# Moving a weight load and its product forward in the first batches of a Linformer and mixture-of-experts kernel

## The chip, the cores and the metric

One core of a Trainium2 chip runs the whole program. The metric is device time in microseconds (us); less is better.

## The reference

An attention with 32 memory slots feeds a mixture of experts. In short:

```python
a = softmax(phi, over the 32 slots)                  # B, H, S, 32
k_m = einsum('bhsm,bhsd->bhmd', a, k)                # slot sums of the keys
v_m = einsum('bhsm,bhsd->bhmd', a, v)                # and of the values
attn = softmax(q @ k_m.T / sqrt(64))                 # B, H, S, 32
x = (attn @ v_m) as tokens of 512                    # 8 heads x 64
expert = argmax(normalised x @ normalised emb.T / tau); gate = its softmax weight
out = gate * (relu(x @ w1[expert]) @ w2[expert])     # 512 -> 1024 -> 512
```

There are 8 batches of 576 tokens, 8 heads of 64, 8 experts, all in float32.

## The kernel before

The kernel goes batch by batch. For each batch it forms the slot sums of keys and values (a softmax of phi on ScalarE, transposes of it on TensorE, products with the loaded keys and values), then the scores and their softmax, then picks an expert, and then runs the two expert layers. The values are never multiplied out to tokens before the first layer: `project` multiplies the slot values by W1 (products `pg`, 512 hidden columns at a time), and `first` multiplies the attention weights by that projection (products `ph`). Matrix products whose precision matters are split in a high and a low part: `gh` and `gl` of the projection, `ah` and `al` of the weights (tile `aT`), `hh` and `hl` of the hidden layer, `wh` and `wl` of W2.

From batch 0's first layer on, the loops `first` and `second` emit the big products of one batch, and a table (`steps`) hangs the small work of the next batches between them. Ahead of that stands a prologue, written out by hand in `moe_linformer` (from L1104 on). The change touches the prologue alone. Every engine runs its own instructions in the order in which the program emits them, and all loads named here go through one queue that SyncE (SP) issues in order.

The prologue prepares batch 0 completely up to its first layer, and the slot sums of batch 1. The steps that matter here, with the names the rows use:

- `load_kv(1)`: keys and values of batch 1 in two halves of 1024 KB, tiles `kx` 0 and `kx` 1, and the last 64 tokens (`kl`, 256 KB).
- `pick`: the expert of batch 0, guessed from sums, is read into a register of SP; `load_w1(e, 0)` and `load_w1(e, 1)` then load W1 in two halves of 512 columns (tile `w1s`, 1024 KB each).
- `turn(1, g)` and `tails(1)`: transposes of batch 1's softmaxed phi on TensorE (tiles `te`, `tz`), copied out by ScalarE to `eT` and `kt`.
- `slots(1, ...)`: the slot sums (`acc0t`, `acc`) over five pieces of tokens, in the order 0, 1, 4, 2, 3; pieces 0 and 1 read `kx` 0, piece 4 reads `kl`, pieces 2 and 3 read `kx` 1.
- `scale(1)`, `keys(1)`, `values(1)`: ScalarE scales the sums to `ks`, TensorE transposes them (`tk`, `tv`), ScalarE copies them out.
- `project(0, ..., apart=True)`: a generator, driven by `next(project)`. Its first step emits the products `pg` of W1's first half, the next one the copies to `gh` on ScalarE and the subtractions to `gl` on VectorE; the second half follows inside `first`.
- `t.attend()` and `t.turned(...)`: products `po` and transposes `tt` of batch 0, after which the first `ph` comes.
- `warm`: products of ones whose result nobody reads; they stand in TensorE's queue between other steps.

Of the kernel before, what the change touches and what calls it, by code (L numbers as in the profile page):

```python
# [19 lines left out]
P = 128  # L20
# [285 lines left out]
class Kernel:  # L306
# [150 lines left out]
                else:  # L457
                    (self.nc.scalar if b in (3, 4) else self.nc.sync).dma_start(to, self.phiT[b, :, g])

    def load_kv(self, b):  # L460
        if 1 < b < B:
            for g in range(NG):
                to, x = self.kl[64 * g : 64 * g + 64], self.kvt[b, :, 4 * g : 4 * g + 4]
                self.nc.sync.dma_start(to, x)
        if b < B:
            for k in range(2):
                if b < 2 and k:
                    x = self.kvt[b].rearrange("t (g j) d -> (t g) (j d)", g=NG)
                    self.nc.sync.dma_start(self.kl.rearrange("p j d -> p (j d)"), x)
                self.nc.sync.dma_start(self.kx[k], self.kv[b, :, 2 * k : 2 * k + 2])  # L470

    def load_q(self, b, halves=(0, 1)):
        if b < B:
# [280 lines left out]
    def project(self, n, vT, room=None, apart=False):  # L754

        nc = self.nc
        for k in range(2):
            ps = [(room or self.mm)([P, 512], f"pg{n}_{k}{g}") for g in range(NG)]
            for g, j, r, c, i in self.heads():
                f = slice(512 * k, 512 * k + 512)  # L760
                nc.tensor.matmul(ps[g][j], lhsT=vT[r, g, c % 2, i], rhs=self.w1s[r, c, f], start=True, stop=True)
            f = slice(512 * k, 512 * k + 512)
            if apart and not k:
                yield
            for g in range(NG):
                nc.scalar.copy(self.gh[:, g, f], ps[g])  # L766
            for g in range(NG):
                nc.vector.tensor_tensor(  # L768
                    out=self.gl[:, g, f], in0=ps[g], in1=self.gh[:, g, f].bitcast(F32), op=ALU.subtract
                )  # L770
            yield
# [331 lines left out]
@with_exitstack  # L1103
def moe_linformer(ctx, tc, phiT, qT, kv, kvt, emb, tau, w1, w2, out):  # L1104
    k = Kernel(ctx, tc, phiT, qT, kv, kvt, emb, tau, w1, w2, out)
    ctx.enter_context(tc.manual_schedule(engines={ET.PE, ET.DVE, ET.Activation, ET.SP, ET.Pool}))


    k.eights()
    k.warm(4)  # L1110
    k.warm(8, hot=k.mm([P, 256], "half", 0))
    k.warm(32, hot=k.mm([P, 64], "cool", 0))
    k.load_phi(0)
    k.load_kv(0)
    k.load_q(0, (0,))
    k.load_router()
    k.consts()
    accs = [k.ps.tile([P, 2 * D], F32, tag=f"{n}3", name=f"acc0{n}", bufs=1) for n in "tm"]
    for vT in k.vT:
        k.nc.vector.memset(vT, 0.0)  # L1120
    router = k.router()
    for g in range(NG):
        k.largest(0, g)
        k.softmax(0, (g,))
    for g in range(NG):
        k.turn(0, g)
        if not g:
            next(router)
        k.warm(4 if g else 8, hot=k.mm([P, 256], f"half{g}", 0))
    k.tails(0)  # L1130
    k.shares(0)
    next(router)
    k.load_phi(1, (0,))
    k.load_q(0, (1,))
    k.load_phi(1, (1,))
    t = Tokens(k, 0, k.pt)
    for ks in ((0, 1), (4,), (2, 3)):
        k.slots(0, accs, ks=ks, first=0 in ks, last=3 in ks)
        if 3 not in ks:
            k.warm(4, hot=k.mm([P, 128], f"hot{ks[0]}", 0))  # L1140
    k.scale(0)
    next(router, None)
    k.warm(2, hot=k.mm([P, 128], "hot2", 0))
    k.load_kv(1)
    k.keys(0)
    t.summed()
    k.again()
    values = k.values(0, copy=k.nc.scalar.copy, room=lambda *a: k.mm(*a, 3))
    all, tr, te = slice(0, BL), [k.mm([P, S - 64], f"tr0_{g}", g) for g in range(NG)], [k.mm([P, 64], "te0_0", 2)]
    k.score(0, tr, 64, S, (0,))  # L1150
    t.guess()
    k.score(0, te, 0, 64, (0,))
    next(values)
    t.fill((0,), slice(2, BL), tr)
    e = t.pick()
    t.fill((0,), slice(0, 2), te)
    list(values)
    k.load_w1(e, 0)
    k.load_w1(e, 1)
    k.load_q(1, (0,))  # L1160
    tl = [k.pt([P, D + E], f"tl0_{g}") for g in range(NG)]
    k.squares(0, tl)
    k.score(0, tr, 64, S, (1,))
    te.append(k.pt([P, 64], "te0_1"))
    k.score(0, te, 0, 64, (1,))
    k.products(0, copy=True)
    work = [t.weigh((g,), all, None if g else k.nc.gpsimd) for g in range(NG)]
    next(work[0])
    for g in range(NG):
        k.largest(1, g)  # L1170
    next(work[0])
    t.fill((1,), slice(2, BL), tr)
    t.fill((1,), slice(0, 2), te)
    k.softmax(1, (0,))
    list(work[0])
    k.softmax(1, (1,))
    k.warm(12, hot=k.mm([P, 256], "warm0", 3))
    list(work[1])
    k.turn(1, 0)
    k.warm(12, hot=k.mm([P, 128], "warm1", 3))  # L1180
    k.turn(1, 1)
    k.tails(1)
    k.warm(10, hot=k.mm([P, 128], "warm2", 3))
    k.shares(1, v=k.nc.gpsimd, invert=False)
    project = k.project(0, k.vT[0], apart=True)
    accs = [accs[0], k.mm([P, 2 * D], "acc1", 3)]
    for ks in ((0,), (1,), (4,), (2,), (3,)):
        k.slots(1, accs, ks=ks, first=0 in ks, last=3 in ks)
    t.divide(range(NG), all, True, lambda: k.invert(1))
    k.tags, k.turns = 4, 3  # L1190
    k.scale(1)
    k.again(k.nc.scalar.copy)
    k.keys(1, lambda *a: k.mm(*a, 3))
    list(k.values(1, copy=k.nc.scalar.copy, room=lambda *a: k.mm(*a, 2)))
    next(project)
    t.turn(range(NG), all)
    for g in range(NG):
        k.part(g, slice(0, HS), k.nc.gpsimd.tensor_copy)
    next(project)
    t.attend()  # L1200
    t.turned(0, 1)
    t.turned(4)
    k.load_w2(e)
    k.load_q(1, (1,))
    k.load_phi(2)
    k.second_part = project
    for b in range(B):
        u = Tokens(k, b + 1, k.pt) if b < B - 1 else None
        left = k.batch(b, t, u)
        t = u  # L1210
    k.rest(*left)
# [29 lines left out]
```

## Time and profile before

| | us |
|---|---|
| median of 3 runs | 393.63 |
| lowest and highest | 392.93, 394.96 |
| the profiled execution | 393.70 |
| its span, first to last instruction | 391.9 |
| TensorE busy in the span | 383.1 (98%) |
| VectorE, ScalarE, GpSimd busy | 242.6, 213.1, 190.0 |

The profile is one execution. Its own time is 1.8 us longer than the span of its instructions. Times in rows count from the span's start. PE is TensorE's products, DVE VectorE, ACT ScalarE, POOL GpSimd, SPq the queue of SyncE. A float32 product is two instructions in the trace where the program has one; transposes are one.

### The profile page before, as it was taken

Reading aid. Unit: us, or ns where it says so; the run is one execution under the profiler, and the core shown is the slowest. Engines: PE = TensorE matmul, PEld = TensorE weight load, DVE = VectorE, ACT = ScalarE, POOL = GpSimd, SP = SyncE. Lnnn points to the kernel's source line nnn. Section 1 sums busy time; section 2 is a strip of 40 time slices with the busy share of each in tenths; the row PEclk is TensorE's granted clock in tenths of the full one; section 3 lists DMA queues with packets and bytes.
Section 4 is the critical chain, followed back from the end, with each engine's and each line's share of the span. In section 5 each row is a group of like instructions: output and inputs, shape, how many; then the busy total and the mean of one; then the engine's idle time right before and its main releaser. Section 6 shows DMA issues by size and latency. Waiting matters only on the chain. (4 is left out here: it accounts for less than half of the span.)

```text
span 391.9 us, 10402 instructions
## 1 busy us (share of the span) xinstructions
PE 383.1 (98%) x3890; PEld 313.7 (80%) x3890; DVE 242.6 (62%) x800; ACT 213.1 (54%) x665; POOL 190.0 (48%) x234
## 2 busy tenths in 40 slices
PE   8899999999999999999999999999999999999995
PEld 5568878799787978889787987879787897879783
DVE  5579896679673798259862798538861696445000
ACT  5366734778484875666656675657641751145011
POOL 1165940596154932478052951559242871529300
PEclk9999999999999999999999999999999999999999
DMA  8999827995789937995489926995379205890011
GB/s 307 407 355 359 347 59 191 339 370 225 162 264 369 403 95 151 382 391 200 90 251 378 403 72 155 349 390 210 74 205 386 91 2 103 271 381 2 30 54 44
DMA packets 65447, 91.25 MB, mean 233 GB/s; under 512 B 40712, under 2 KB 45320, under 8 KB 63216
## 3 DMA queue, kind: packets, MB, share of 16 engines
q1 hardware_dynamic: 62016, 81.02, 61.4%
q0 software_dynamic: 2688, 8.26, 5.8%
q10 hardware_dynamic: 688, 1.26, 1.2%
q8 instruction: 32, 0.52, 0.6%
q14 instruction: 23, 0.19, 0.2%
HBM read 71.19 MB, written 19.33 MB: 231 GB/s over the span
## 5 line engine op out<-in xcount | busy, mean ns | idle before, releaser
L784 PE MATMUL ph<-aT,gh 128*128 128x288 f32 x512 | 103.1, 297 | 0.0
L824 PE MATMUL py<-wh,hh 128*128 128x512 f32 x256 | 100.9, 394 | 0.0
L824 PE MATMUL py<-wl,hh 128*128 128x512 f32 x256 | 99.9, 390 | 0.2 <-POOLq L1013 0.2
L824 PE MATMUL py<-wh,hl 128*128 128x512 f32 x256 | 99.9, 390 | 0.0
L751 POOL TENSOR_TENSOR wl<-w2s,wh 128x512 fp32r<-128x512 f32 x64 | 83.2, 1300 | 5.1
L784 PEld LDWEIGHTS ph<-aT,gh 128*128 128x128 f32 x512 | 81.8, 188 | 1.8 <-DVE hl L791 0.8
L784 PE MATMUL ph<-aT,gl 128*128 128x288 f32 x256 | 75.4, 295 | 0.0
L788 ACT ACTIVATE hh<-ph 128x224 fp32r<-128x224 f32 (+1 forms) x128 | 48.8, 388 | 33.7 <-PE ph L784 33.0
L791 DVE SCALAR_TENSOR_TENSOR hl<-ph,hh 128x224 fp32r<-128x224 f32 (+1 forms) x128 | 51.8, 417 | 23.5 <-ACT hh L788 16.9
L829 ACT ACTIVATE ys<-py,gate 128x512 f32<-128x512 f32 (+1 forms) x40 | 25.7, 643 | 63.3 <-PE py L824 33.0
L990 POOL DMA_DIRECT2D out_dram<-ys x28 | 16.2, 580 | 89.6 <-ACT ys L829 89.5
L824 PEld LDWEIGHTS py<-wh,hh 128*128 128x128 f32 x256 | 48.1, 188 | 10.9 <-issue 1.4
L824 PEld LDWEIGHTS py<-wh,hl 128*128 128x128 f32 x256 | 48.1, 188 | 10.2
L824 PEld LDWEIGHTS py<-wl,hh 128*128 128x128 f32 x256 | 48.1, 188 | 10.1 <-POOLq L1013 0.6
L784 PEld LDWEIGHTS ph<-aT,gl 128*128 128x128 f32 x256 | 48.0, 188 | 0.0
L768 DVE TENSOR_TENSOR gl<-pg,gh 128x512 fp32r<-128x512 f32 x32 | 20.0, 684 | 43.4 <-ACT gh L766 43.4
L750 POOL CAST wh<-w2s 128x512 fp32r<-128x512 f32 x62 | 41.3, 665 | 0.9 <-PE ph L784 0.8
L741 POOL TENSOR_TENSOR aT<-aw,aT 128x576 fp32r<-128x576 f32 (+1 forms) x18 | 23.5, 1320 | 34.1 <-DVE aT L740 29.3
L579 ACT COPY eT<-xt 32x256 f32<-32x256 f32 x80 | 32.3, 403 | 1.4
L813 PE MATMUL py<-w2s,h 128*64 128x256 f32 x256 | 29.4, 382 | 0.0
L651 ACT COPY kv<-kt 32x64 f32<-32x64 f32 x96 | 23.3, 243 | 6.6 <-DVE kt L641 5.5
L813 PEld LDWEIGHTS py<-w2s,h 128*64 128x64 f32 x256 | 17.7, 137 | 10.7 <-DVE aw L102 2.1
(184 smaller groups left out, 473.8 us busy)
## 6 DMA issues: line engine op xcount, KB each, us to landing
kx<-kv SPq DMA_DIRECT2D x16, 1024.0 KB, 11.3
w2s<-w SPq DMA_DIRECT2D x28, 512.0 KB, 10.1
w1s<-w SPq DMA_DIRECT2D x28, 512.0 KB, 6.3
qt<-qT SPq DMA_DIRECT2D x14, 576.0 KB, 10.1
out_dram<-ys POOLq DMA_DIRECT2D x28, 256.0 KB, 6.4
ad<-aw SPq DMA_DIRECT2D x8, 576.0 KB, 12.8
td<-x SPq DMA_DIRECT2D x56, 72.0 KB, 2.5
ea<-td SPq DMA_DIRECT2D x7, 512.0 KB, 4.1
```

The lines of the kernel that those rows point to most:

```text
L579: nc.scalar.copy(eT[to, :8, m].rearrange("p (g k) m -> p g k m", g=NG), xt[at, :, q : BL - 2 : 4])
L651: nc.scalar.copy(y, self.kt[32 * l : 32 * l + 32, g, h + 2 * i :: 2 - 4 * i])
L741: self.nc.gpsimd.tensor_tensor(out=al, in0=a, in1=ah.bitcast(F32), op=ALU.subtract)
L750: (copy or self.nc.scalar.copy)(h, x)
L751: self.nc.gpsimd.tensor_tensor(out=l, in0=x, in1=h.bitcast(F32), op=ALU.subtract)
L768: nc.vector.tensor_tensor(out=self.gl[:, g, f], in0=ps[g], in1=self.gh[:, g, f].bitcast(F32), op=ALU.subtract)
L784: nc.tensor.matmul(p, lhsT=w[:, g, fs], rhs=x[:, g, to], start=g == 0 and k == 0, stop=g == 1 and k == 2)
L788: nc.scalar.activation(self.hh[:, f, at], q, AF.Relu)
L791: nc.vector.scalar_tensor_tensor(out=self.hl[:, f, at], in0=q, scalar=0.0, in1=self.hh[:, f, at].bitcast(F32), op0=ALU.max, op1=ALU.subtract)
L813: nc.tensor.matmul(p[64 * j : 64 * j + 64], lhsT=self.h4[:, f], rhs=self.w2s[:, f, d * j : d * j + d], start=f == 0, stop=f == 7,)
L824: nc.tensor.matmul(p, lhsT=h[:, f, to], rhs=w[:, f], start=f == 0 and k == 0, stop=f == 7 and k == 2)
L829: nc.scalar.activation(y[:, :d], p, AF.Copy, scale=gate[:, i : i + 1])
```

## The change

Four things move in the prologue, and one generator gets another step.

- `load_kv` takes the halves to load. Batch 1's `kx` 0 and `kl` are loaded where they were; `kx` 1 is loaded after the pick, behind W1's first half and ahead of its second.
- The products `pg` of W1's first half stand between piece 4 and piece 2 of the slot sums. The copies to `gh` stand behind the slot sums, and the subtractions to `gl` where both stood before.
- The first transposes of batch 1's phi are emitted ahead of the exponential of batch 0's second half of scores, so that ScalarE copies them out sooner.
- Ten `warm` products ahead of the slot sums go.
- Eight opening `warm` products of 256 columns become sixteen of 128.

```diff
-    def load_kv(self, b):
+    def load_kv(self, b, ks=range(2)):
...
         if b < B:
-            for k in range(2):
-                if b < 2 and k:
+            for k in ks:
+                self.nc.sync.dma_start(self.kx[k], self.kv[b, :, 2 * k : 2 * k + 2])
+                if b < 2 and not k:
                     x = self.kvt[b].rearrange("t (g j) d -> (t g) (j d)", g=NG)
                     self.nc.sync.dma_start(self.kl.rearrange("p j d -> p (j d)"), x)
-                self.nc.sync.dma_start(self.kx[k], self.kv[b, :, 2 * k : 2 * k + 2])
...
             for g in range(NG):
                 nc.scalar.copy(self.gh[:, g, f], ps[g])
+            if apart and not k:
+                yield
...
-    k.warm(8, hot=k.mm([P, 256], "half", 0))
+    k.warm(16, hot=k.mm([P, 128], "half", 0))
...
-    k.load_kv(1)
+    k.load_kv(1, (0,))
...
     k.load_w1(e, 0)
+    k.load_kv(1, (1,))
     k.load_w1(e, 1)
...
     k.warm(12, hot=k.mm([P, 256], "warm0", 3))
+    k.turn(1, 0)
     list(work[1])
-    k.turn(1, 0)
     k.warm(12, hot=k.mm([P, 128], "warm1", 3))
     k.turn(1, 1)
     k.tails(1)
-    k.warm(10, hot=k.mm([P, 128], "warm2", 3))
...
     for ks in ((0,), (1,), (4,), (2,), (3,)):
+        if 2 in ks:
+            next(project)
         k.slots(1, accs, ks=ks, first=0 in ks, last=3 in ks)
+    next(project)
...
     list(k.values(1, copy=k.nc.scalar.copy, room=lambda *a: k.mm(*a, 2)))
-    next(project)
     t.turn(range(NG), all)
```

SP's queue, from the load of batch 1's `kx` 0 to W1's second half; `TENSOR_LOAD ai` reads the picked expert. Before:

```order
L470 DMA kx0_70<-kv 128x2048
L469 DMA kl_72<-kvt 128x512
L470 DMA kx1_71<-kv 128x2048
L229 TENSOR_LOAD ai_354
L229 ISA x2
L489 ISA
L489 DMA w1s_87<-w1 128x4x512
L489 ISA
L489 DMA w1s_87<-w1 128x4x512
```

And with the change:

```order
L467 DMA kx0_70<-kv 128x2048
L470 DMA kl_72<-kvt 128x512
L229 TENSOR_LOAD ai_361
L229 ISA x2
L489 ISA
L489 DMA w1s_87<-w1 128x4x512
L467 DMA kx1_71<-kv 128x2048
L489 ISA
L489 DMA w1s_87<-w1 128x4x512
```

The load of `kx` 1 has gone from ahead of the register read to between the two halves of W1.

TensorE, from piece 2 of batch 1's slot sums to the first product of `attend`. Before:

```order
L602 MATMUL acc0t_182<-kx1_71,eT_74 32x128 x4
L602 MATMUL acc1_477<-kx1_71,eT_74 32x128 x4
L602 MATMUL acc0t_182<-kx1_71,eT_74 32x128 x4
L602 MATMUL acc1_477<-kx1_71,eT_74 32x128 x4
L627 MATMUL tk1_0_529<-ident_162,ks_75 128x128 x2
L662 MATMUL tv1_0_533<-ident_162,ks_75 128x128 x2
L761 MATMUL pg0_00_540<-w1s_87,kv20_78 32x512 x4
L761 MATMUL pg0_01_541<-w1s_87,kv20_78 32x512 x4
L133 MATMUL po0_0_562<-vv_80,aw_86 64x72
```

And with the change, from behind piece 4:

```order
L761 MATMUL pg0_00_499<-w1s_87,kv20_78 32x512 x4
L761 MATMUL pg0_01_500<-w1s_87,kv20_78 32x512 x4
L602 MATMUL acc0t_190<-kx1_71,eT_74 32x128 x4
L602 MATMUL acc1_474<-kx1_71,eT_74 32x128 x4
L602 MATMUL acc0t_190<-kx1_71,eT_74 32x128 x4
L602 MATMUL acc1_474<-kx1_71,eT_74 32x128 x4
L627 MATMUL tk1_0_538<-ident_170,ks_75 128x128 x2
L662 MATMUL tv1_0_542<-ident_170,ks_75 128x128 x2
L133 MATMUL po0_0_559<-vv_80,aw_86 64x72
```

The products `pg` have moved from between `tv` and `po` to ahead of the pieces that read `kx` 1.

ScalarE, from the exponential of batch 0's second half of scores (`x`) to the copies to `gh`. Before:

```order
L76 ACTIVATE x_81<-x_81 128x576
L546 COPY eT_74<-te1_0_432 128x512
L546 COPY eT_74<-te1_1_451 128x512
L553 COPY kt_76<-tz1_457 128x256
L619 ACTIVATE ks_75<-acc0t_182,rs1_404 128x128
L619 ACTIVATE ks_75<-acc1_477,rs1_404 128x128
L656 COPY ks_75<-ks_75 128x2x64
L632 COPY kv21_79<-tk1_0_529 128x256
L668 COPY kv21_79<-tv1_0_533 64x2x32 x4
L766 CAST gh_91<-pg0_00_540 128x512
L766 CAST gh_91<-pg0_01_541 128x512
```

And with the change:

```order
L546 COPY eT_74<-te1_0_436 128x512
L76 ACTIVATE x_81<-x_81 128x576
L546 COPY eT_74<-te1_1_459 128x512
L553 COPY kt_76<-tz1_465 128x256
L766 CAST gh_91<-pg0_00_499 128x512
L766 CAST gh_91<-pg0_01_500 128x512
L619 ACTIVATE ks_75<-acc0t_190,rs1_412 128x128
L619 ACTIVATE ks_75<-acc1_474,rs1_412 128x128
L656 COPY ks_75<-ks_75 128x2x64
```

One copy to `eT` has passed the exponential, and the two copies to `gh` have passed the scaling of the slot sums.

## Rows read from the trace of the kernel before

**Rows 1.** Windows, TensorE: stretch, length, busy, granted clock, DMA share, GB/s

```profile
30.42:387.30 356.88, 356.55 (x3441) 1.00 0.68 225
```

**Rows 2.** Timeline of TensorE, prologue's end: start, length, line, operation, idle before

```profile
22.35 0.72 PE L442 MATMUL warm<-ones 128*128 128x128 bf16 x10
23.41 0.43 PE L602 MATMUL acc0t<-kx,eT 128*32 128x128 f32 x8 [0.34 <-ACT eT L546]
23.90 0.42 PE L602 MATMUL acc<-kx,eT 128*32 128x128 f32 x8
...
25.02 0.42 PE L602 MATMUL acc0t<-kx,eT 128*32 128x128 f32 x8
...
26.66 0.44 PE L627 MATMUL tk<-ident,ks 128*128 128x128 f32 x2 [0.56 <-ACT ks L619]
...
27.36 1.09 PE L761 MATMUL pg<-w1s,kv 64*32 64x512 f32 x16
28.38 1.48 PE L133 MATMUL po<-vv,aw 64*64 64x72 f32 x80
...
30.42 0.51 PE L784 MATMUL ph<-aT,gh 128*128 128x288 f32 x2
...
32.17 1.09 PE L761 MATMUL pg<-w1s,kv 64*32 64x512 f32 x16
```

**Rows 3.** Timeline of ScalarE in the same stretch

```profile
22.07 0.68 ACT L76 ACTIVATE x<-x 128x576 f32<-128x576 f32 x1 [0.74 <-DVE x L74]
22.77 1.07 ACT L546 COPY eT<-te 128x512 f32<-128x512 f32 x2
...
25.93 0.37 ACT L619 ACTIVATE ks<-acc0t,rs 128x128 f32<-128x128 f32 x1 [1.81 <-DVE aw L102]
...
28.48 1.07 ACT L766 CAST gh<-pg 128x512 fp32r<-128x512 f32 x2 [0.16 <-PE pg L761]
```

**Rows 4.** Timelines of VectorE and GpSimd: what the first `ph` also needs

```profile
26.71 0.20 DVE L102 STREAM_TRANSPOSE aw<-x 128x64 f32<-128x64 f32 x1
29.11 1.29 DVE L768 TENSOR_TENSOR gl<-pg,gh 128x512 fp32r<-128x512 f32 x2 [2.19 <-ACT gh L766]
...
27.67 0.80 POOL L741 TENSOR_TENSOR aT<-aw,aT 128x288 fp32r<-128x288 f32 x1
```

**Rows 5.** SP's timeline, then DMA issues by window (size, us to landing)

```profile
13.83 0.33 SPq L470 DMA_DIRECT2D kx<-kv  x1
18.47 1.50 SPq L489 DMA_DIRECT2D w1s<-w  x2
...
kx<-kv SPq DMA_DIRECT2D x1, 1024.0 KB, 8.7
...
w1s<-w SPq DMA_DIRECT2D x1, 1024.0 KB, 6.8
...
w1s<-w SPq DMA_DIRECT2D x1, 1024.0 KB, 8.5
```

**Rows 6.** Windows, all engines: last three columns are granted clock, DMA share, GB/s

```profile
1.50:3.70 2.20, 2.14 (x8) 0.91 (x7) 1.34 (x9) 1.49 (x2) 0.27 (x2) 1.00 0.92 275
...
19.70:19.90 0.20, 0.20 (x4) 0.18 (x3) 0.20 (x1) 0.20 (x3) 0.00 (x0) 1.00 0.10 41
19.90:23.10 3.20, 3.17 (x39) 2.73 (x36) 3.04 (x6) 2.43 (x6) 1.67 (x6) 1.00 0.95 342
23.10:25.80 2.70, 2.32 (x78) 2.06 (x80) 2.58 (x7) 1.02 (x3) 1.84 (x3) 1.00 1.05 394
```

**Rows 7.** Timelines: the opening, VectorE's first use of a load, later warm products

```profile
2.97 1.87 PE L442 MATMUL half<-ones 128*128 128x256 bf16 x8
...
9.58 0.65 PE L602 MATMUL acc0t<-kx,eT 128*32 128x128 f32 x16 [0.66 <-DMA kx<-kv]
...
3.67 1.51 DVE L504 TENSOR_REDUCE nm<-ex 128x1 f32<-128x576 f32 x2 [0.83 <-DMA ex<-phiT]
...
19.08 1.49 PE L442 MATMUL warm<-ones 128*128 128x256 bf16 x12
```

## Prediction

> **What bounds the kernel now.** I read the windows first. From the first `ph` at 30.42 us to 387.30 us TensorE is busy 356.55 of 356.88 us [rows 1]: what stands behind 30.42 us is TensorE's own work, none of it changed, and whatever the prologue gains or loses at the first `ph` arrives undiminished at the end. So the question is one number: at what time does the first `ph` start?
>
> The timeline of TensorE around it [rows 2] shows the chain. The slot sums of batch 1 start at 23.41 us, after 0.34 us of waiting for ScalarE's copy `eT`. The second group follows at 23.90, the pieces that read `kx` 1 at 25.02, the transposes `tk` at 26.66 after 0.56 us of waiting for `ks`, `pg` at 27.36, `po` at 28.38 and `ph` at 30.42. All the idle time in it, 0.90 us, is TensorE waiting for ScalarE. ScalarE's timeline [rows 3] gives the other half: it stands idle 0.74 us before the exponential at 22.07, makes two copies to `eT` from 22.77 (1.07 us), scales the first sums at 25.93 and starts `gh` at 28.48, again 1.07 us for two.
>
> The loads come last. `kx` 1 is issued at 13.83 and lands 8.7 us later, at 22.5; the halves of W1 are issued at 18.47 and about 19.4 and land after 6.8 and 8.5 us, at 25.3 and 27.9 [rows 5]. Each is there before TensorE asks for it (25.02 for `kx` 1, 27.36 and 32.17 for the halves of W1 [rows 2]), so no load is on the path now.
>
> **The change, part by part.** *Copy and warm products.* With the first copy to `eT` in the idle 0.74 us ahead of 22.07, only the second is left behind the exponential: it ends about 23.30 instead of 23.84. The first sums no longer wait behind the ten warm products (0.72 us from 22.35 [rows 2]); the second group then starts about 23.37 instead of 23.90, which is 0.53 us sooner. Its two pieces and piece 4 take the 1.12 us that stand between 23.90 and 25.02. TensorE is ready for the moved `pg` at 24.49. Removing the warm products alone is worth nothing, since the copies set this time.
>
> *The product.* `pg` fills 27.36 to 28.38, that is 1.02 us of the queue [rows 2]. It leaves that place and takes the same 1.02 us at 24.49, so that piece 2 could start at 25.51. Behind it, from the start of piece 2 to the scaling on ScalarE stand 0.91 us (25.02 to 25.93), and from there to the end of `tv` 1.43 us (25.93 to 27.36) [rows 2, 3]. `po` then follows at once.
>
> *The copies to `gh`* now stand in ScalarE's queue ahead of the scaling. They can start when `pg` ends: 1.12 us after its start by the rows (27.36 to 28.48). With the 1.07 us that they take, the scaling can't start before 24.49 + 2.19 = 26.68 us. Without any wait for loads the path is therefore: scaling at 26.68, `po` at 28.11, 0.27 us sooner than 28.38. Behind the scaling wait `tk`, `tv` and with them TensorE's whole queue. The subtractions to `gl` follow VectorE's last transpose of `aw`, which ends at 26.91, and take 1.29 us; GpSimd's `al` is done at 28.47 [rows 4]. Both are there before any `ph` considered here (30.1 or later), so they cost nothing; if `gl` lost its 1.9 us of cover it would hold `ph` itself.
>
> *The loads* decide the rest. W1's first half can't be issued sooner, since SP still waits for the pick: 18.47. In the profile of before, the mean DMA share falls to 0.10 from 19.70 to 19.90 and the rate to 41 GB/s [rows 6]: the queue had run dry, so most engines began W1's first half when its issue let them, not when `kx` 1 did. Taking `kx` 1 from ahead of it leaves the DMA engines idle earlier and brings W1's bytes hardly sooner. What it does take away is the tail: `kx` 1 landed at 22.5, 2.6 us after the share had fallen, so a few engines must have run late, and those kept W1's landing at 25.3 too. The bytes themselves (1.05 MB) were through by 23.1 (342 GB/s x 3.2 us = 1.09 MB), and a second 1.05 MB by 25.8 (394 x 2.7 = 1.06 MB) [rows 6]. How soon a load lands behind its last byte when no engine is late is seen at the start: 0.6 MB have moved by 3.7 us (275 GB/s x 2.2 us), as much as the first two loads of phi, and VectorE uses the first of them from 3.67 us [rows 6, 7]; the second reduction can have started by 4.4. That is up to about 0.5 us. So W1's first half lands between 23.2 and 25.3; I take 23.6, before `pg` wants it. Behind it stands `kx` 1 in the place of W1's second half: between 25.6 (no late engine, some rate regained) and 27.9 (late engines stay as late as they were). I take 25.8 + 0.5 = 26.3, since after a pause of more than 2 us in the queue the late ones should have caught up.
>
> By the Trainium skill ("DMA: Bandwidth & Descriptors", section on why a DMA increments its semaphore by 16 and not by 1) a load counts as landed only when the last of its up to 16 engines has finished. The gap between the idle share at 19.8 and the landing at 22.5 agrees with it.
>
> *Sum.* Piece 2 starts at 26.35, the scaling at 26.35 + 0.91 = 27.26, `po` at 27.26 + 1.43 = 28.69. Against 28.38 that is 0.31 us later. `ph` moves from 30.42 to 30.73, the span from 391.9 to 392.2, the profiled 393.70 to 394.0. The median of the runs shown is 0.07 us below the profiled time, so I predict **393.9 us**. In short: the reordering is worth 0.27 us, and TensorE gives it back by waiting 0.8 us for `kx` 1.
>
> *What is hidden.* W1's second half lands 2.6 us behind `kx` 1, about 28.9 and 30.5 at worst, before 32.17. Everything SP issues behind it moves by one issue of 0.33 us at most, and the bytes by about 1 us; I see no use of them that stands closer than W1's second half. Sixteen opening products of 128 columns have as many columns as eight of 256; if each cost 0.03 us of its own more, the first transposes would come 0.25 us later, and TensorE then waits 0.66 us for `kx` at 9.58 anyway [rows 7]. That cover must go before it costs anything.
>
> **The rivals.**
>
> *The loads arrive in time.* If `kx` 1 lands by 25.7, ScalarE's queue is the limit and `po` comes at 28.11: 0.27 us gained, 393.4 us. For it: the bytes of two loads would be through by 25.8 even at the rates of before, and their start was slow. Against it: landing must then come with the last byte. Chance 0.2.
>
> *The late engines stay late* (the other side: slower). If they lag for a reason of their own and not for what stood in their queue at the start, `kx` 1 lands where W1's second half did, at 27.9. Piece 2 starts at 27.95, the scaling at 28.86, `po` at 30.29: 1.91 us lost, 395.5 us. It loses from a landing after 26.0 on, the point at which `po` comes at 28.38 again. For it: the landings of before are 2.6 to 2.8 us apart, a steady 1 MB pace without a pause at 19.8. Against it: the pause is longer now. Chance 0.13.
>
> *TensorE slows down.* It loses ten warm products and gains up to three pauses between 22.6 and 28: 0.75 us before the second group, 0.8 us for `kx` 1, 0.7 us for `ks`. The opening's 256-column products took 1.87 us for eight, the later ones 1.49 us for twelve [rows 7], nearly twice the time each, with the granted clock printed as 1.00; before, pauses of 0.66 and 0.56 us [rows 2, 7] brought no such slow products. If the pace halves from piece 2 to the first `ph` (slot pieces 0.9, `tk` and `tv` 0.7, `po` and the transposes 2.04 us), 3.6 us of work would cost up to 3.6 more, with a middle of 2.5: 396.4 us. Chance 0.07. The Trainium skill ("TensorE: Matmul & The Clock Gate", section on HAM oscillation) says that waits for a load between short groups of products can bring the array back to its lower clock, 1.2 of 2.4 GHz; no stretch of this trace shows that after the opening.
>
> **How the numbers follow.** The forecast (a small loss, -0.2 to +1.0 us, 393.5 to 394.6) has 0.60, the rivals 0.20, 0.13 and 0.07. The three runs shown spread over 2 us, so the range must hold that spread as well as the first two rivals and part of the third's: 392.8 to 395.6. What a measurement here can tell from no change is about 0.5%, 2 us: faster needs less than 391.7, which no case reaches (0.02 for what I overlooked); slower needs more than 395.6, which the last rival gives and the late engines nearly do (0.09). The rest, 0.89, is no change.
>
> **What would show it.** In the changed profile: `pg` behind piece 4 near 24.5 with no wait, or a wait for `w1s`; a wait of TensorE for `kx` of 0.8 us ahead of piece 2; ScalarE's `eT` copy near 21.3 and `gh` from 25.6; `tk` near 28.0, `po` near 28.7 and the first `ph` near 30.7; landings of W1's first half near 5.1 us and of `kx` 1 near 7 us after their issue. The prediction is wrong if `kx` 1 lands at 27.9, if `po` or `ph` run at half pace, or if `ph` starts where I say and the end moves by something else.

## The result: slower, by a load that lands late and a clock that falls

| | before | changed |
|---|---|---|
| median of 16 runs each, us | 393.12 | 396.21 |
| lowest and highest | 391.86, 394.96 | 393.31, 398.28 |
| ratio, 95% interval | | 1.0072, 1.0048 to 1.0095 |
| the profiled execution | 393.70 | 397.29 |
| its span | 391.9 | 395.5 |

The forecast was 393.9 us and no change. The kernel is slower by more than the 0.5% that can be told from nothing, and above the range. The windows of TensorE in the changed kernel, from the twelve late `warm` products to piece 2, the wait itself, piece 2 to the first `ph`, and what follows (start:end, length, busy, granted clock, DMA share, GB/s):

```profile
18.59:27.39 8.80, 6.21 (x103) 1.00 0.87 300
25.43:27.39 1.96, 0.00 (x1) 1.00 0.97 369
28.39:34.10 5.71, 5.14 (x99) 0.50 1.03 404
27.39:34.10 6.71, 6.14 (x123) 0.55 1.03 403
34.10:390.90 356.80, 356.65 (x3440) 1.00 0.67 223
```

Behind the first `ph` hardly anything has changed: 356.65 of 356.80 us are busy, against 356.55 of 356.88 in [rows 1]. The first `ph` itself starts at 34.10 in place of 30.42, 3.7 us later, and the span is 3.6 us longer. So the loss lies in the prologue, and the windows show two parts of it: an idle stretch of 1.96 us, and 5.7 us at a granted clock of 0.50, the lower of the engine's two levels (1.2 of 2.4 GHz), where it stays for 0.85 us behind the first `ph` too. The profiled execution is one of the slower ones, 1.1 us above the median. The timeline of TensorE names both parts:

```profile
18.59 1.49 PE L442 MATMUL warm<-ones 128*128 128x256 bf16 x12
...
24.34 1.09 PE L761 MATMUL pg<-w1s,kv 64*32 64x512 f32 x16 [0.23 <-DMA w1s<-w]
...
27.39 0.43 PE L602 MATMUL acc0t<-kx,eT 128*32 128x128 f32 x8 [1.96 <-DMA kx<-kv]
...
29.25 0.69 PE L627 MATMUL tk<-ident,ks 128*128 128x128 f32 x2 [0.57 <-ACT ks L619]
...
30.30 2.68 PE L133 MATMUL po<-vv,aw 64*64 64x72 f32 x80
32.91 1.54 PE L165 MATMUL tt<-ident,aw 128*128 128x128 f32 x6
34.10 0.83 PE L786 MATMUL ph<-aT,gh 128*128 128x288 f32 x2
```

`pg` starts about where the forecast had it (24.34) and waits 0.23 us for W1. Piece 2 waits 1.96 us for `kx` 1 instead of 0.8. Then the same 80 products `po` take 2.68 us that took 1.48 in [rows 2], and `tk` 0.69 instead of 0.44. SP's timeline and the DMA issues (KB, us from issue to landing) give the reason of the wait:

```profile
17.99 0.72 SPq L489 DMA_DIRECT2D w1s<-w  x1
18.81 1.17 SPq L467 DMA_DIRECT2D kx<-kv  x1
...
w1s<-w SPq DMA_DIRECT2D x1, 1024.0 KB, 6.3
...
kx<-kv SPq DMA_DIRECT2D x1, 1024.0 KB, 8.5
```

The second megabyte behind the pick lands 8.5 us after its issue, at 27.3. In [rows 5] W1's second half, which stood in that place of the queue, took 8.5 as well.

**A measure that leaves the start out.** The twelve late `warm` products start at 19.08 us in the profile of before and between 16.9 and 19.0 in the others. This is the run's doing: e6_turn_only and e10_turn_keep_warm, which differ from before only behind that row, have it at 17.74 and 17.20. So the profiles are compared from the start of that row: to the start of the first `acc0t` of piece 2 (A), from there to the first `ph` (B), and both together. Each number is a difference of two starts in TensorE's timeline. The last columns are the ratio to before on the same chip, from all runs, and the granted clock over B.

| kernel | A | B | A + B | against before | clock in B | ratio (95%) |
|---|---|---|---|---|---|---|
| before | 5.94 | 5.40 | 11.34 | | 1.00 | |
| changed | 8.80 | 6.71 | 15.51 | +4.17 | 0.55 | 1.0072 (1.0048, 1.0095) |
| e11_change_again | 8.67 | 5.72 | 14.39 | +3.05 | 0.70 | 1.0091 (1.0060, 1.0121) |
| e14_change_beside | 8.78 | 4.40 | 13.18 | +1.84 | 1.00 | 1.0081 (1.0054, 1.0107) |
| e1_loads_back | 7.38 | 4.50 | 11.88 | +0.54 | 1.00 | 1.0022 (1.0000, 1.0044) |
| e2_product_back | 10.43 | 8.83 | 19.26 | +7.92 | 0.52 | 1.0139 (1.0084, 1.0193) |
| e9_swap | 10.67 | 7.00 | 17.67 | +6.33 | 0.53 | 1.0112 (1.0068, 1.0156) |
| e8_warm_back | 9.80 | 7.13 | 16.93 | +5.59 | 0.52 | 1.0115 (1.0076, 1.0153) |
| e12_half_fill | 9.11 | 5.86 | 14.97 | +3.63 | 0.71 | 1.0085 (1.0052, 1.0119) |
| e3_fill | 8.50 | 4.40 | 12.90 | +1.56 | 1.00 | 1.0102 (1.0061, 1.0143) |
| e5_fill_again | 9.11 | 4.40 | 13.51 | +2.17 | 1.00 | 1.0068 (1.0047, 1.0088) |
| e13_fill_beside | 8.33 | 4.39 | 12.72 | +1.38 | 1.00 | 1.0075 (1.0047, 1.0103) |
| e4_opening | 5.94 | 5.40 | 11.34 | 0.00 | 1.00 | 1.0020 (0.9999, 1.0040) |
| e6_turn_only | 5.32 | 5.40 | 10.72 | -0.62 | 1.00 | 0.9961 (0.9939, 0.9983) |
| e15_turn_again | 5.32 | 5.39 | 10.71 | -0.63 | 1.00 | 0.9966 (0.9945, 0.9986) |
| e10_turn_keep_warm | 5.31 | 5.40 | 10.71 | -0.63 | 1.00 | 0.9989 (0.9964, 1.0014) |
| e7_behind_sums | 5.32 | 5.94 | 11.26 | -0.08 | 1.00 | 0.9985 (0.9961, 1.0008) |

Where `pg` stands ahead of piece 2 its 1.02 us are in A, elsewhere in B; without them B is 4.38 us in before. In e9_swap `pg` itself runs at the lower clock, within A.

### The profile page after: what moved, and what is told of

Same layout as the page of the kernel before. It is cut to its first block, busy times and chain, and to the rows that moved or that the text cites. A ratio compares the mean times of both kernels' runs of the same rounds, so it can differ in the third digit from the quotient of the medians.

```text
span 395.5 us, 10396 instructions
## 1 busy us (share of the span) xinstructions
PE 384.5 (97%) x3888; PEld 315.3 (80%) x3888; DVE 242.6 (61%) x800; ACT 213.4 (54%) x665; POOL 190.3 (48%) x234
## 5 line engine op out<-in xcount | busy, mean ns | idle before, releaser
L831 ACT ACTIVATE ys<-py,gate 128x512 f32<-128x512 f32 (+1 forms) x40 | 25.7, 644 | 63.5 <-PE py L826 33.9
```

The costliest lines, as they stand in the source:

```text
L831: nc.scalar.activation(y[:, :d], p, AF.Copy, scale=gate[:, i : i + 1])
```

## Experiments

### The load or the product

e1_loads_back puts the load of `kx` 1 back ahead of the pick and keeps everything else of the change.

```diff
-    k.load_kv(1, (0,))
+    k.load_kv(1)
...
-    k.load_kv(1, (1,))
```

> The changed kernel with the load of kx 1 back ahead of the pick; the product pg stays between the slot sums. Theory (the loss is the wait for kx 1 and the slow clock that follows it): no wait for kx, no stretch of granted clock 0.5, the first ph between 30.0 and 30.8 us, and a time within 0.8 us of the kernel before (about 393), with a wait of up to 1 us for W1 ahead of pg. Rival (the place of pg, with the gh copies ahead of the scaling, costs it): still about 396, the first ph after 33 us.

Measured: 393.39 us against 392.97, ratio 1.0022. TensorE's timeline has no wait for `kx` 1 any more, and one for W1:

```profile
24.43 1.09 PE L761 MATMUL pg<-w1s,kv 64*32 64x512 f32 x16 [0.84 <-DMA w1s<-w]
25.45 0.42 PE L602 MATMUL acc0t<-kx,eT 128*32 128x128 f32 x8
...
29.95 0.51 PE L786 MATMUL ph<-aT,gh 128*128 128x288 f32 x2
```

The first `ph` comes 0.54 us later than before by the table, and the clock stays at 1.00. So the place of the load makes most of the loss; the product at its new place is no gain by itself either, mainly because W1's first half comes 0.84 us after TensorE asks for it.

e2_product_back keeps the change's loads and puts `pg` and the copies to `gh` back behind the values.

```diff
-        if 2 in ks:
-            next(project)
         k.slots(1, accs, ks=ks, first=0 in ks, last=3 in ks)
-    next(project)
...
     list(k.values(1, copy=k.nc.scalar.copy, room=lambda *a: k.mm(*a, 2)))
+    next(project)
+    next(project)
```

> The changed kernel with pg and its copies back behind the values, the loads in the changed order. Theory: TensorE waits 3 us or more for kx 1 at piece 2, from about 24.0 to 27.3 us, the clock falls after it, and the time is that of the change or above it (396 to 398). Rival (loads harmless): 393, no wait above 1 us.

Measured: 398.35 us, ratio 1.0139. Here `kx` 1 landed 10.2 us after its issue. One row of the timeline, one window over B:

```profile
27.62 0.66 PE L602 MATMUL acc0t<-kx,eT 128*32 128x128 f32 x8 [4.90 <-DMA kx<-kv]
...
27.62:36.45 8.83, 8.25 (x139) 0.52 1.02 388
```

Nothing stands between piece 4 and piece 2, TensorE waits 4.90 us, and all that follows up to the first `ph` runs at half clock. The product between the sums is a cover for the late load, not the cause of the loss.

e9_swap moves `kx` 1 ahead of W1's first half, still behind the pick.

```diff
-    k.load_w1(e, 0)
     k.load_kv(1, (1,))
+    k.load_w1(e, 0)
     k.load_w1(e, 1)
```

> The changed kernel with kx 1 loaded behind the pick but ahead of W1's first half. Theory (whatever 1 MB is issued second behind the pick lands about 9 us after its issue, and TensorE needs both by 25.5 us): kx 1 now lands about 6 to 7 us after its issue, W1's first half about 9, so TensorE waits 2 to 3 us for W1 at pg and not at all for kx, and the time stays 395.5 to 397.5. Rival (kx 1 itself, or what stands behind W1, is what is slow): one of the two waits is gone and nothing takes its place, 394 or less.

Measured: 397.2 us against 392.23, ratio 1.0112. Now `kx` 1 lands 5.1 us after its issue and `pg` is the one that waits:

```profile
27.43 1.96 PE L761 MATMUL pg<-w1s,kv 64*32 64x512 f32 x16 [3.26 <-DMA w1s<-w]
...
27.43:36.32 8.89, 8.31 (x139) 0.52 1.03 408
```

Whichever of the two loads is second behind the pick lands at 27.3 or 27.4 in these two profiles, and the products that need it wait. The order of the two only chooses who waits.

### The clock

e3_fill puts sixteen `warm` products of 256 columns, whose result nobody reads, between `pg` and piece 2. e5_fill_again and e13_fill_beside are the same kernel again, e12_half_fill has eight.

```diff
         if 2 in ks:
             next(project)
+            k.warm(16, hot=k.mm([P, 256], "fill", 2))
```

> The changed kernel with sixteen warm products of 256 columns (1.8 us) between pg and piece 2, where TensorE stood idle. Theory (idle time before the fall costs the clock, some 2.1 us of the loss): kx 1 lands as late as before, the granted clock stays at 1.00 through the prologue, and the time falls by 1.5 to 2.3 us to about 394. Rival (the clock falls for another reason, or its fall costs nothing): 396 as the change.

> The kernel of the run with sixteen warm products ahead of piece 2, once more: its four times (395.4 to 397.2) don't go with its profile, in which the granted clock stayed at 1.00 and the first ph came at 30.69 us. If the clock is worth what the profiles say, the median lies between 393.5 and 395.5. If it is 396 or more again, the warm products give back no time on average, and the profile must show where else 2 us go (behind the first ph, or at the end).

> The changed kernel with eight warm products of 256 columns ahead of piece 2, half of the idle time. Theory: the clock stays at 1.00 in most runs, and the median is 0.5 to 1.5 us below that of the changed kernel beside it. Rival (the slow clock is worth nothing on average, or half of the idle time is enough for the fall): no difference.

> The change with sixteen warm products of 256 columns behind pg, now beside the unfilled change on the same chip. If the lower clock costs about 2 us on average (as in the profiled run of the change, where the stretch from tk to the first ph took 2.1 us longer), this kernel takes 394.5 to 395.5 us when the change takes 396 to 397, and its runs all show a mean clock of 0.997 or more. If the wait for kx 1 is nearly all of the loss, the two lie within 0.8 us of each other.

e11_change_again and e14_change_beside are the changed kernel itself, on the chips of e12_half_fill and e13_fill_beside.

> The changed kernel itself, on the same chip as the next one, so that the two can be compared. 1.007 of the kernel before; in the profile a wait for kx 1 of 1 to 3 us, and a stretch of granted clock 0.5 behind it if the wait is 1.5 us or more.

> The changed kernel itself. Of its 22 runs so far 7 had a mean clock of 0.998 or more and took 394.9 us on average, the other 15 took 396.7. If the clock makes that difference, the runs here fall into the same two groups, 1 to 2.5 us apart, and the kernel filled lies with the upper clock's group. If the clock only goes along with a later load, the filled kernel has as many runs above 396 as this one.

Measured: 396.38, 395.35 and 395.86 us filled, 396.03 with half the fill, 396.1 and 395.24 without. In all three filled profiles the granted clock over B is 1.00 and B is 4.39 or 4.40 us. From e13_fill_beside:

```profile
25.16 1.92 PE L442 MATMUL fill<-ones 128*128 128x256 bf16 x16
...
27.02:31.41 4.39, 3.81 (x123) 1.00 1.05 413
```

Half the fill left a wait of 1.56 us in its profile, and the clock fell (0.71 over B); its five other runs stand at a mean clock of 0.997 or more and take 395.4 us on average. But e14_change_beside shows the change without a fill and without a fall:

```profile
24.02 1.09 PE L761 MATMUL pg<-w1s,kv 64*32 64x512 f32 x16 [0.49 <-DMA w1s<-w]
26.79 0.43 PE L602 MATMUL acc0t<-kx,eT 128*32 128x128 f32 x8 [1.67 <-DMA kx<-kv]
...
29.14 1.48 PE L133 MATMUL po<-vv,aw 64*64 64x72 f32 x80
31.19 0.52 PE L786 MATMUL ph<-aT,gh 128*128 128x288 f32 x2
...
26.79:31.19 4.40, 3.82 (x123) 1.00 1.03 390
```

The same program, nearly the same waits, and `po` takes 1.48 us as before. In e11_change_again the clock fell for a part of B:

```profile
27.62:33.34 5.72, 5.14 (x122) 0.70 1.04 412
```

This splits the loss of the profiled executions. A is 8.67 to 8.80 us in all three profiles of the change, and with B at full clock the first `ph` comes 1.84 us late: that is the load. B is 4.40, 5.72 and 6.71 us at 1.00, 0.70 and 0.55 of the clock: the fall costs 0, 1.3 and 2.3 us on top.

What the fall is worth on average I could settle only between bounds. Sorted by mean clock, the seven of the 30 runs of the change at 0.991 or less take 397.3 us on average, the thirteen at 0.993 to 0.996 396.2 and the ten at 0.998 or more 394.9; all 30 take 396.0. So a lower mean clock goes with a longer time, and the fall costs at most about 1.1 us on average, less if a later load brings both. The 17 filled runs, 15 of them at 0.997 or more, take 395.7, and on the one chip that ran both the ratios are 1.0075 and 1.0081. (A mean of 0.997 needs no fall in the prologue: each profile also ends at 0.50, behind TensorE's last product. In e3_fill that is the last 2.68 us, with TensorE idle.)

In its profiles the filled kernel loses 1.4 to 2.2 us up to the first `ph`; its runs lose about 3. The difference lies behind the first `ph`, where the span goes on for 362.3 to 363.5 us in the filled profiles and 361.4 to 362.7 in those of the change. In two of the three filled profiles it lies at the very end. The last store (ScalarE's queue, us to landing) in e5_fill_again and in e3_fill:

```profile
out_dram<-ys ACTq DMA_DIRECT2D x1, 64.0 KB, 2.3
...
out_dram<-ys ACTq DMA_DIRECT2D x1, 64.0 KB, 3.7
```

It takes 3.1 us in e13_fill_beside and 2.2 or 2.3 in all other profiles. From the first `ph` to the end of TensorE's last product the filled kernel takes 357.0 to 357.5 us, the change 356.6 to 357.9. Whether the fill has a part in the later stores, no run shows. As measured the fill is no remedy, and the clock's share of the average loss lies between 0.3 us (filled against unfilled, within the noise) and 1.1 us.

e8_warm_back puts the ten `warm` products ahead of the slot sums back.

```diff
     k.tails(1)
+    k.warm(10, hot=k.mm([P, 128], "warm2", 3))
```

> The changed kernel with the ten warm products back ahead of the slot sums. If the wait for kx 1 alone lets the clock fall, nothing changes: 396, with a stretch of 0.5 in the profile when the wait is as long. If their removal let it fall, the clock stays at 1.00 and the time goes to about 394.5.

Measured: 397.17 us, ratio 1.0115; the clock falls all the same (0.52 over B), behind waits of 1.74 us for W1 and 1.46 us for `kx` 1. Taking these products away is not what lets the clock fall.

### The parts alone

e4_opening: before, with sixteen opening products of 128 columns in place of eight of 256.

```diff
-    k.warm(8, hot=k.mm([P, 256], "half", 0))
+    k.warm(16, hot=k.mm([P, 128], "half", 0))
```

> The kernel before with nothing but the sixteen opening products of 128 columns. If the opening is what brought the first transposes 0.71 us sooner in the changed kernel's profile, they start near 5.6 us here too; whether anything of it reaches the end depends on the first load of kx, at which TensorE waits anyway. Theory: loads set it, so 393 as before, within 0.5 us. Rival: 0.5 us faster.

Measured: 393.27 us, ratio 1.0020, and A + B, which starts behind the opening, is 11.34 as in before. The first transposes start at 6.56 us here and in e14_change_beside, at 6.33 in before and 5.62 in the first profile of the change, so the 0.71 us were the run's doing. No gain from the opening shows.

e6_turn_only: before, with the early transposes and without the ten `warm` products. e15_turn_again repeats it; e10_turn_keep_warm keeps the ten.

```diff
-    list(work[1])
     k.turn(1, 0)
+    list(work[1])
...
-    k.warm(10, hot=k.mm([P, 128], "warm2", 3))
```

> The kernel before with the early first transposes and without the ten warm products, nothing else. Theory: the second group of slot sums starts 0.5 us sooner behind the last transposes, W1's first half then arrives just as pg wants it, and 0.2 to 0.5 us come through: 392.5 to 392.9. Rival (the warm products kept the clock): a stretch of granted clock 0.5 between 20 and 36 us and 1 us or more slower.

> Before with the early copy to eT and without the ten warm products, once more. If the gain of 0.3 to 0.5 per cent is real: 390.5 to 391.8 us, ratio 0.995 to 0.998. If it was the draw of the runs: 0.999 to 1.001.

> The kernel before with the early first transposes and all ten warm products. Theory: the sooner copy alone gives the gain, since the warm products end at 23.1 us, ahead of the second copy: the first ph comes 0.5 to 0.7 us sooner behind the first late warm product, and the time is 0.1 to 0.4% below the kernel before. Rival: the warm products hold the sums back, and half or more of the gain is lost.

Measured: 391.07, 391.57 and 392.35 us. In all three piece 2 starts 0.62 or 0.63 us sooner; in e15_turn_again:

```profile
18.48 1.48 PE L442 MATMUL warm<-ones 128*128 128x256 bf16 x12
...
23.80 0.43 PE L602 MATMUL acc0t<-kx,eT 128*32 128x128 f32 x8
...
29.19 0.52 PE L784 MATMUL ph<-aT,gh 128*128 128x288 f32 x2
```

With the ten products left in, the prologue gains the same 0.63 us, so in the prologue they are worth nothing. The ratios 0.9961 and 0.9966 lie below 1 with their whole intervals. They are more than the 0.63 us of the prologue (0.16%) would give, which lies at the very end of the intervals (0.9983 and 0.9986); e10_turn_keep_warm, at 0.9989, fits it. The early copy without the ten products has the lowest ratios of this case, below before and below the change; whether it gains more than the 0.63 us stays open.

e7_behind_sums: the change with the loads as before, `pg` directly behind all slot sums and the copies to `gh` behind the scaling.

```diff
-    k.load_kv(1, (0,))
+    k.load_kv(1)
...
-    k.load_kv(1, (1,))
...
-        if 2 in ks:
-            next(project)
...
     k.again(k.nc.scalar.copy)
+    next(project)
     k.keys(1, lambda *a: k.mm(*a, 3))
```

> Loads as in the kernel before, early transposes, sixteen opening products, no ten warm products, and pg behind all slot sums, ahead of tk, with the gh copies behind the scaling. Theory: pg fills TensorE's wait for the scaling (0.56 us) without a wait for a load above 0.5 us; the first ph comes 0.6 to 1.1 us sooner than in the kernel before, measured from the first of the late warm products, and the time is 392.0 to 392.5. Rival: W1 lands too late for it, and nothing is gained.

Measured: ratio 0.9985. `pg` waits 0.95 us for W1 and takes back what the early copy had gained: A is 0.62 us shorter, B 0.54 us longer. Behind the values, as in e6_turn_only, `pg` finds W1 there.

## Why the prediction was wrong

*The path.* "Whatever the prologue gains or loses at the first `ph` arrives undiminished": right. The first `ph` came 3.68 us later and the span grew by 3.6.

*The early copy, the ten products, the opening.* Forecast 0.53 us sooner, nothing, nothing; measured 0.62 us, and no gain or loss from the other two. Right.

*The product and the copies to `gh`.* The 1.02 us moved as forecast. The copies end before the late sums do, so they limit nothing in the change. In e1_loads_back, where they do, ScalarE starts them at 25.56 and the scaling right behind them at 26.52, that is 2.09 us after `pg` starts; the forecast said 2.19. Right.

*W1's first half.* Forecast to land 5.1 us after its issue, measured 5.2 to 6.7 in the profiles of the change and the filled kernels. Too early by up to 1.6 us, which costs at most 0.6 us of waiting there. In e8_warm_back and e2_product_back, with the same order of loads, it took 7.8 and 8.4.

***`kx` 1, the step that failed.*** "I take 25.8 + 0.5 = 26.3, since after a pause of more than 2 us in the queue the late ones should have caught up." The pause was there, and the 0.5 us held: the last packet of `kx` 1 ends at 27.02 in the trace's DMA records, and the load counts as landed 0.3 us later, at 27.3. What failed is the term 25.8, by which the bytes of both loads were to be through (25.3 on the scale of the changed profile). From issue to landing `kx` 1 took 8.5 us, not 7, also in e11_change_again (8.4) and e14_change_beside (8.5). Windows of the changed kernel, in the columns of the first fence:

```profile
17.00:19.50 2.50, 2.50 (x39) 1.00 0.13 44
19.50:22.00 2.50, 2.50 (x32) 1.00 0.94 324
22.00:24.00 2.00, 1.60 (x49) 1.00 0.94 268
24.00:27.30 3.30, 1.21 (x21) 1.00 0.96 371
```

Add up the bytes (1.46 MB up to 24.0, then 371 GB/s), and 2.10 MB, as many as both loads have, are through by 25.7. But such a sum takes all bytes of the queue for those of two loads. W1's rows are 2 KB and go in packets of 2 KB, those of `kx` are 8 KB, and each load ends with sixteen packets of 4 bytes, as many as there are DMA engines. So the counts of packets by size tell the loads apart, from 19.50 to 25.70 us and from 25.70 to 27.30:

```profile
DMA packets 654, 1.97 MB, mean 318 GB/s; under 512 B 22, under 2 KB 22, under 8 KB 544
...
DMA packets 250, 0.60 MB, mean 376 GB/s; under 512 B 10, under 2 KB 10, under 8 KB 232
```

At 25.7 us 18 of the 128 packets of `kx` 1 had not begun and ten of its sixteen end packets were still to come; up to the landing 222 packets of 2 KB, W1's second half, went beside them. So the engines were out of step, and the DMA records show two parts of it, in shares that differ. The last of the sixteen end packets of W1's first half came behind the other fifteen: by 1.1 us in the changed profile, 1.5 in e14_change_beside, 2.7 in e8_warm_back, not at all in e11_change_again. And packets of `kx` 1 were slow: 14 took 0.6 to 1.35 us in the changed profile, ten up to 1.37 in e11_change_again, none over 0.55 in e8_warm_back; the longest in before took 0.33. So the late engine can catch up after a pause, as the forecast said, and `kx` 1 comes late even so. Why packets were slow, and why the engine catches up in one profile and not in another, no run shows.

The rival "the late engines stay late" had the right size: it put piece 2 at 27.95, 8.87 us behind the row at 19.08, and the loss at 1.91 us; A is 8.67 to 8.80 and the loss at full clock 1.84. Since slow packets made up for the engine that caught up, that fit is in part luck. It had a chance of 0.13 because I reasoned about why engines were late, when [rows 5] already had the price: 8.5 us for the second megabyte behind the pick.

*The clock.* The other slow rival was right in mechanism and near in size: up to 3.6 us with a middle of 2.5, against 1.3 and 2.3 in two profiles and nothing in the third. The error was to set it beside the late load with a chance of its own (0.07). The fall follows the wait: of the seven profiles in which `kx` 1 or W1 kept TensorE idle for 1.56 to 4.90 us six have it; with the load back or the wait filled none has. A longer wait made both likely together, 395.5 and more, and the range ended at 395.6. The Trainium skill ("TensorE: Matmul & The Clock Gate", section on HAM oscillation) has this coupling, a wait for a load that brings the next products back to the lower clock; the traces agree, but for e14_change_beside, where a wait of 1.67 us did not.

*The sum.* 30.73 for the first `ph` was 30.24 on the scale of the changed profile, whose late `warm` products start 0.49 us sooner. It came at 34.10, 3.86 later: 1.53 of it the load (1.84 less the 0.31 forecast), 2.33 the clock.

## What to carry to other kernels

Price a moved load first by the load that stood in that place of the queue, not by its bytes: the row of its neighbour, 8.5 us, was the answer here (8.1 to 8.9 in seven of the nine profiles with this order of loads, 9.5 and 10.2 in e8_warm_back and e2_product_back), and the byte count was 1.5 us too kind. A window's GB/s counts every load in the queue; packet sizes tell which of them moved. When a change adds a wait to the engine that sets the end, forecast the slower clock behind it as part of the same case, not as a separate accident. And try the parts of a change alone: a copy that stood sooner was worth 0.63 us of the prologue and was hidden under a load that cost more than twice that.

## What the runs showed of the hardware

- SP's issue of `kx` 1 directly behind W1's first half took 1.17 us (1.12 to 1.27 in its repeats and the filled kernels, but 0.56 in e8_warm_back and e2_product_back, with the same order), against 0.33 for the same load ahead of the pick in [rows 5]; its landing is counted from its start.
- In the changed kernel's profile the granted clock was 1.00 through the wait for `kx` 1 and for 0.73 us of products behind it, and 0.50 from 28.12 to 34.95 us, of which TensorE was busy 6.26 us. In e2_product_back and e9_swap, with waits of 4.90 and 3.26 us, it was 0.50 from 25.78 and 25.70 us on, still within the wait.
- The same program kept its clock in one profile of three, with waits for `kx` 1 of 1.96, 2.13 and 1.67 us (the last kept it; with the waits for W1 they are 2.19, 2.13 and 2.16). What decides it, I don't know.
